# Whole stores, two queues of units and four unequal zero transfers at the end of a decode step's backward pass

## The chip, the cores and the metric

The kernel runs on one core of a Trainium2 chip. The core has five instruction queues that run side by side and meet only at semaphores: TensorE (PE, matrix products; its weight loads are listed apart as PEld), VectorE (DVE), ScalarE (ACT), GpSimd (POOL) and SyncE (SP). All five can ask for DMA transfers, and the transfers run on 16 DMA engines, which move data between the chip's main memory (HBM, here "dram") and the core's on-chip memory (SBUF). PE writes its results to PSUM, from where DVE or ACT copies them to SBUF; such a copy is called an eviction here.

The metric is the device time of one execution in microseconds: the median of several executions. The kernel before has 450.68 us, from three executions between 450.56 and 451.15.

## The reference

The reference is one decode step (one token, batch 1) through two layers that share their weights, and its gradients. Cut to what matters:

```python
def _A_ref(x, k_cache, v_cache, wq, wo):            # attention over the last W = 4096 cache rows
    q = (x @ wq).reshape(1, 1, 32, 128)             # 32 heads, 4 groups of the cache, 8 heads for each
    k = k_cache[:, :, Sk - W:, :]; v = v_cache[:, :, Sk - W:, :]      # Sk = 32768
    p = softmax(q k^T * 128 ** -0.5)
    return (p v).reshape(1, 1, 4096) @ wo

def _B_ref(x, w1, b1, w2):                          # MLP, 1024 -> 3584 -> 1024
    h = x @ w1 + b1
    return (h * tanh(softplus(h))) @ w2

x = x + _A_ref(_layernorm(x), ...); x = x + _B_ref(_layernorm(x), ...)
x = x + _A_ref(_layernorm(x), ...); x = x + _B_ref(_layernorm(x), ...)

_out, _vjp = jax.vjp(f, A_x, A_k_cache, A_v_cache, A_wq, A_wo, B_w1, B_b1, B_w2)
return (_out, *_vjp(grad_out))
```

There are nine outputs, all in bf16: out_0 is the step's result, out_1 the gradient of x, out_2 and out_3 those of the key and value caches (4 groups x 32768 rows x 128 each), out_4 that of wq (1024 x 4096), out_5 of wo (4096 x 1024), out_6 of w1 (1024 x 3584), out_7 of b1 and out_8 of w2 (3584 x 1024). In out_2 and out_3 only the last 4096 rows of each group are computed; the 28672 rows before them are zeros, which the kernel has to write. With two tokens' worth of vectors (one for each layer's pass), the gradient of a weight matrix is a sum of two outer products.

## The kernel before, in words

**The passes.** The kernel first runs the four layers forward, then backward. Since there is one token, every product is a matrix times a vector, and the weights are streamed through the chip: wq and wo as tiles of 128 x 4096 bf16 (1 MB), w2 likewise, w1 kept in SBUF. Tiles go through a ring of eight buffers. `Ring.pump` (L71) issues the load of the next tile on SP as soon as a buffer is free. The last load of the run is that of wq for the backward pass of the first attention layer, "the last pass of wq": eight tiles, in `attn_bwd`, whose loop calls the hook `dn1(t)` after tile t.

**The zeros.** `zeros(n)` (L265) takes n pieces from the list `zjobs` and issues each as a transfer on POOL. A piece is 128 partitions x 4096 bf16, that is 128 rows of 8 KB, 1 MB, from the tile `zt`, which holds zeros. The calls stand at chosen places of the passes, most of them behind a tiny POOL copy (L260) that waits for a value of that place. The last calls are `zeros(4)` in `dp1` and `dq1`, `zeros(2)` in `dn1` at t = 3, and `zeros(4)` behind `attn_bwd`; the last piece of the list is a half.

**Rows for the outer products.** The vectors are needed as rows in one partition each, in `ROWS` (in the memory of w1, no longer needed then): partitions 0 and 1 for wq's gradient, 32 and 33 for wo's, 64 and 65 for w1's, 96 and 97 for w2's. Some are put to HBM earlier (`put_by`) and fetched by POOL with `take_back` (L836), others are turned by PE and ACT (`rowize`, and `rowize_f` for b1's gradient) and sent into place by `rows_go` (L1041), on POOL for three of them and on SP for the last. `twins` (L1070) copies them on SP to the partitions 32 away, into `TWIN`, so that PE can take two products from two sets of partitions.

**The units.** A unit (`unit_dw`) is one or two outer products 128 x 512 into one of four PSUM tiles `wide` (L1078) and one eviction by DVE (L313) or ACT (L316), whichever has the smaller sum of estimated costs, into a staging buffer of 128 x 4096. `units_rows` and `units_cols` are generators that yield after each unit; `units_kv` does the same for the computed cache rows with 32-row products (L1129). They stand in four queues `todo[0]` to `todo[3]`, and `work(n)` takes n units from the queues in turn. All units run after the last pass of wq: 16 units, the end of the gradient of x (`g0_rest`) and the two small stores out_0 and out_1, 32 units, and then the rest with the cache gradients mixed in.

**The stores.** After each unit `store` decides whether to issue a transfer on SP. With a full buffer it stores what is not yet sent (L1050). For the first eight buffers, for the last buffer of each matrix and for all cache buffers it also sends the first half as soon as it is there (L1055). A buffer that was sent goes back to `stage_free`.

**Semaphores of transfers.** Eight semaphores serve SP's transfers in turn and eight POOL's, so the issue of a transfer also waits until the one eight places before it has landed.

Of the kernel before, what the change touches and what calls it, by code (L numbers as in the profile page):

```python
# [15 lines left out]
P = 128  # L16
HQ = 32
DH = 128
# [3 lines left out]
G = 4  # L22
# [71 lines left out]
def kernel(  # L94
# [943 lines left out]
    def rows_go(queue):  # L1038

        while rows_out:  # L1040
            queue.dma_start(*rows_out.pop(0))  # L1041


    def store(dst, s, old, new, of, last):


        h = (of + 1) // 2
        if new == of:
            lo = sent.pop(id(s), 0)
            nc.sync.dma_start(dst[:, lo * 512:], s[:, lo * 512:of * 512])  # L1050
            stage_free.append(s)
        elif old < h <= new and wide and (last or len(firsts) < 8):
            firsts.append(0)
            sent[id(s)] = new
            nc.sync.dma_start(dst[:, 0:new * 512], s[:, 0:new * 512])  # L1055

    sent, firsts = {}, []

    def rooms(left):

# [23 lines left out]
    def units_rows(base, nblk, out):  # L1084

        for c in range(nblk // 4):
            s = stage_free.popleft()
            for tt in range(4):
                n = 0
                while n < 2:  # L1090
                    m = unit_dw(base, NOFF + (4 * c + tt) * P, 512 * n, s[:, tt * D + n * 512:(tt + 1) * D], 2 - n)
                    n += m
                    store(out.rearrange("(c p k) d -> p c (k d)", p=P, k=4)[:, c], s, 2 * tt + n - m, 2 * tt + n, 8,
                          c == nblk // 4 - 1)
                    yield

    def units_cols(base, ncol, out):

        for t in range(TD):
            s = stage_free.popleft()  # L1100
            n = 0
            while n < ncol:
                m = unit_dw(base, t * P, NOFF + 512 * n, s[:, n * 512:ncol * 512], ncol - n)
                n += m
                store(out[t * P:(t + 1) * P, :], s, n - m, n, ncol, t == TD - 1)
                yield

    def kv_rows(a, X, Y, YS):
# [13 lines left out]
    def units_kv(a, g, YS, out_t):  # L1122
        s = stage_free.popleft()
        q = 0
        while q < 8:
            b, m = rooms(8 - q)
            for k in range(2 * m):
                tp = 2 * q + k
                nc.tensor.matmul(b[:, k * 256:(k + 1) * 256], lhsT=RT[32 * g:32 * g + 32, a, tp, :],  # L1129
                                 rhs=YS[32 * g:32 * g + 32, :], start=True, stop=True, tile_position=(32 * g, 0))  # L1130
            evac(s[:, q * 512:(q + m) * 512], b[:, 0:512 * m], cost=((0.69, 0.585), (1.23, 0.95))[m - 1])
            q += m
            store(out_t[0, g, ZR:, :].rearrange("(p t) d -> p (t d)", p=P), s, q - m, q, 8, True)
            yield


# [44 lines left out]


    todo[3].append(units_rows(96, TF, out_8))
    todo[2].append(units_cols(64, 7, out_6))
    do1_acc = tmp([P, HQ], FP32, "da")

    def do1(c):
        if c == 1:
            take_back("AC", 96, NOFF, 1)
            take_back("OC", 32, NOFF)  # L1190
            take_back("NB", 64, 0)
            take_back("NA", 0, 0)
        if c == 4:
            y = to_eight(YR, RT.rearrange("p a t s -> p (a t s)")[:, 0:512].bitcast(FP32))
            nc.vector.tensor_tensor(out=x4[:], in0=y, in1=x3[:], op=ALU.add)
        if c == 5:
            rowize(GA, TD, 32, 0)
            rowize(GB, TD, 96, 0)
            rows_go(nc.gpsimd)
            zeros(2)  # L1200
        if c == 6:
            rowize_f()
            rows_go(nc.gpsimd)

    def dp1():
        zeros(4)
# [10 lines left out]
    def dn1(t):  # L1217
# [64 lines left out]
```

## Time and profile before

| | |
|---|---|
| median of 3 executions | 450.68 us |
| the profiled execution: time, span | 450.31 us, 448.5 us |
| mean granted TensorE clock | 0.668 |
| busy of the span | PE 70%, PEld 54%, DVE 58%, ACT 47%, POOL 10% |
| DMA | 181.40 MB, mean 404 GB/s |
| of it on SP's queue q1, on POOL's queue q0 | 122.30 MB, 58.26 MB |
| units' stage | from 334 us to 424 us of the span |
| zero pieces | 55 of 1024 KB and one of 512 KB on POOL, one of 512 KB on SP |

The span is the time from the first to the last record of the profiled execution; 1.8 us of the execution's time lie outside. "Busy" is the time in which an engine works. In the tables of stretches, one line is one stretch of the span: busy time of each engine and, in brackets, the number of instructions; the granted clock of PE; the DMA share, which is the mean busy share of the 16 DMA engines (one engine alone gives 0.06, and two packets of one engine overlap a little, so that a full load shows as 1.01 to 1.03); and GB/s. A line that names SPq is an issue on SP's queue: its start, how long the issue took with all others merged into it, and how many they are.

### The profile page before, as it was taken

How to read it: one execution, taken by the hardware profiler on the slowest of the kernel's cores; microseconds unless marked ns; L12 is line 12 of the kernel's file. 1: busy time of each engine (PE TensorE's matmuls, PEld its weight loads, DVE VectorE, ACT ScalarE, POOL GpSimd, SP SyncE). 2: the span in 40 equal slices, each digit the busy share in tenths (PEclk: the TensorE clock that was granted, in tenths of full speed). 3: DMA queues.
4: the chain of work that ended last, by engine and by line, in shares of the span. 5: the costliest groups of instructions: out<-in, count | busy, mean ns of one | idle time of the engine just before them, and what ended most of it. 6: DMA issues, size and time to landing. Idle time of an engine off the chain costs nothing.

```text
span 448.5 us, 12849 instructions
## 1 busy us (share of the span) xinstructions
PE 314.8 (70%) x5681; PEld 243.3 (54%) x5681; DVE 262.2 (58%) x516; ACT 209.4 (47%) x238; POOL 44.5 (10%) x94
## 2 busy tenths in 40 slices
PE   3835542565698797987987666798877888899600
PEld 3735532445685696986986545798862222234300
DVE  4504746368551664864477447654478998998600
ACT  2501101011058576861474341561348999999700
POOL 1000000001232212102101003023220000000000
PEclk9955555556559799986799657957685555555555
DMA  8999999999999999999999999999999899999994
GB/s 336 422 420 420 419 419 418 418 355 425 400 422 421 422 422 416 397 422 422 424 422 422 427 423 419 405 410 388 405 397 412 347 411 416 416 420 411 409 406 192
DMA packets 30057, 181.40 MB, mean 404 GB/s; under 512 B 3954, under 2 KB 5162, under 8 KB 12082
## 3 DMA queue, kind: packets, MB, share of 16 engines
q1 hardware_dynamic: 21478, 122.30, 66.6%
q0 software_dynamic: 8432, 58.26, 31.5%
q8 instruction: 44, 0.72, 0.6%
q14 instruction: 11, 0.09, 0.0%
q10 hardware_dynamic: 92, 0.02, 0.0%
HBM read 81.84 MB, written 98.62 MB: 402 GB/s over the span
## 4 chain that ended last, share of the span: by engine, by line
DMA 40%; PE 31%; DVE 13%; ACT 5%; issue 4%; SPq 0%; ACTq 0%; DVEq 0%
DMA ring<-in_B_w_dram 13%; PE BIG L489 10%; DMA W<-in_A_wo_dram 9%; DMA ring<-in_A_wq_dram 7%; DMA ring<-in_A_wo_dram 5%; DMA W<-in_B_w_dram 4%; PE TP L508 4%; PE wide L1129 4%; ACT ring L316 3%; PE wide L1078 3%; DVE ring L313 3%; DMA W<-in_A_k_cache_dram 2%; DVE W L313 2%; PE BIG L667 2%; PE MV L956 2%
## 5 line engine op out<-in xcount | busy, mean ns | idle before, releaser
L316 ACT COPY ring<-BIG 128x1024 bf16<-128x1024 bf16 x52 | 51.4, 1014 | 50.0 <-PE BIG L489 30.2
L1078 PE MATMUL wide<-W 2*128 2x512 bf16 x240 | 53.1, 597 | 9.7 <-ACT ring L316 2.4
L489 PE MATMUL BIG<-ident_bf,ring 128*128 128x128 bf16 x672 | 54.5, 234 | 2.0 <-issue 1.2
L489 PEld LDWEIGHTS <-ring 128*128 128x128 bf16 x768 | 51.6, 107 | 3.4 <-issue 2.7
L466 DVE CUSTOM_DVE_ANT_0 junk<-ring,SC 128x1024 bf16<-128x1024 bf16 x32 | 38.9, 1215 | 11.0 <-DMA ring<-in_B_w_dram 10.6
L1078 PEld LDWEIGHTS <-W 2*128 2x128 bf16 x240 | 12.8, 102 | 46.3 <-issue 45.4
L508 PEld LDWEIGHTS <-ring 128*128 128x128 bf16 x864 | 29.9, 98 | 11.7 <-issue 6.3
L316 ACT CAST ring<-wide 128x1024 bf16<-128x1024 f32 (+1 forms) x37 | 34.5, 1015 | 1.1 <-PE wide L1078 1.1
L265 POOL DMA_DIRECT2D out_dram<-zt x56 | 29.9, 538 | 48.8 <-DMA out_dram<-zt 47.9
L313 DVE CAST ring<-wide 128x1024 bf16<-128x1024 f32 (+1 forms) x27 | 31.3, 1198 | 2.8 <-PE wide L1078 2.7
L316 ACT COPY KT<-BIG 128x1024 bf16<-128x1024 bf16 x22 | 21.6, 1007 | 21.8 <-PE BIG L667 19.9
L313 DVE COPY ring<-BIG 128x1024 bf16<-128x1024 bf16 x32 | 21.8, 689 | 15.1 <-PE BIG L489 12.5
L466 DVE CUSTOM_DVE_ANT_0 junk<-ring,DSX 128x1024 bf16<-128x1024 bf16 x24 | 29.4, 1224 | 0.8
L489 PE MATMUL BIG<-ident_bf,W 128*128 128x128 bf16 x280 | 26.9, 255 | 3.1 <-DMA W<-in_A_wo_dram 2.7
L316 ACT COPY W<-BIG 128x1024 bf16<-128x1024 bf16 x20 | 20.1, 1014 | 11.8 <-PE BIG L489 11.6
L551 PE MATMUL MV<-NA,ring 128*128 128x1 bf16 x512 | 15.3, 165 | 13.4 <-DMA ring<-in_A_wq_dram 12.1
L489 PEld LDWEIGHTS <-W 128*128 128x128 bf16 x288 | 21.6, 123 | 3.5 <-DMA W<-in_A_wo_dram 2.9
L551 PEld LDWEIGHTS <-ring 128*128 128x128 bf16 x512 | 14.7, 104 | 14.2 <-DMA ring<-in_A_wq_dram 12.8
L1129 PE MATMUL wide<-W 32*128 32x256 bf16 x128 | 19.7, 403 | 1.5 <-DVE KT L313 0.9
L316 ACT CAST KT<-wide 128x1024 bf16<-128x1024 f32 x19 | 19.1, 1030 | 1.6 <-PE wide L1129 1.1
L316 ACT CAST W<-wide 128x1024 bf16<-128x1024 f32 x16 | 16.0, 1024 | 6.6 <-PE wide L1078 6.2
L354 PE MATMUL YR<-ring,AC 128*32 128x256 bf16 x208 | 10.9, 367 | 11.1 <-DMA ring<-in_B_w_dram 8.7
(279 smaller groups left out, 524.5 us busy)
## 6 DMA issues: line engine op xcount, KB each, us to landing
out_dram<-zt POOLq DMA_DIRECT2D x55, 1024.0 KB, 20.7
ring<-in_A_wq_dram SPq DMA_DIRECT2D x24, 1024.0 KB, 12.8
ring<-in_A_wo_dram SPq DMA_DIRECT2D x14, 1024.0 KB, 19.0
ring<-in_B_w_dram SPq DMA_DIRECT2D x13, 1024.0 KB, 18.9
W<-in_A_wo_dram SPq DMA_DIRECT2D x10, 1024.0 KB, 19.9
out_dram<-ring SPq DMA_DIRECT2D x15, 512.0 KB, 11.1
W<-in_B_w_dram SPq DMA_DIRECT2D x8, 896.0 KB, 18.4
out_dram<-ring SPq DMA_DIRECT2D x5, 1024.0 KB, 12.3
```

The source lines that it names most:

```text
L265: nc.gpsimd.dma_start(dst, zt[:, 0:dst.shape[1]])
L313: nc.vector.tensor_copy(dst, src)
L316: nc.scalar.copy(dst, src)
L354: nc.tensor.matmul(bank[32 * j:32 * j + 32, 0:n].rearrange("p (g a) -> p g a", a=m.shape[-1]), lhsT=vec.to_broadcast([P, 32]), rhs=m, star ...
L466: nc.vector.tensor_tensor_reduce(out=out, in0=a, in1=vec, scale=1.0, scalar=acc if i else 0.0, op0=ALU.mult, op1=ALU.add, accum_out=acc)
L489: nc.tensor.transpose(b[:, i * P:(i + 1) * P], block(w, i) if block else w[:, i * P:(i + 1) * P], ident_bf[:])
L508: nc.tensor.matmul(out, lhsT=w[:, i * P:(i + 1) * P], rhs=rhs_of(i), start=fresh[0], stop=last and i == n - 1, skip_group_check=True)
L551: nc.tensor.matmul(q_ps[:, h:h + 1], lhsT=ch[:, h * P:(h + 1) * P], rhs=NA[:, t, l:l + 1], start=(k == 0 and h == 0), stop=(k == TD - 1), ...
L667: nc.tensor.transpose(b[:, i * P:(i + 1) * P], T[:, g, 8 * b8 + i, :], ident_bf[:])
L956: nc.tensor.matmul(dq_ps[:, g_ * 8:g_ * 8 + 8], lhsT=KT[:, g_, t, :], rhs=DSX[:, c:c + 8], start=(g_ == 0 and t == 0), stop=(t == TS - 1), ...
L1078: nc.tensor.matmul(b[:, 512 * i:512 * i + 512], lhsT=R[at:at + 2, lo:lo + P], rhs=R[at:at + 2, ro + 512 * i:ro + 512 * i + 512], start=Tru ...
L1129: nc.tensor.matmul(b[:, k * 256:(k + 1) * 256], lhsT=RT[32 * g:32 * g + 32, a, tp, :], rhs=YS[32 * g:32 * g + 32, :], start=True, stop=Tru ...
```

## The change

Five things are changed.

1. `store` issues one transfer for each buffer, when it is full. The halves of before (the lists `sent` and `firsts`) are gone. The buffers, the units and their evictions stay.
2. w1's units follow w2's in `todo[3]`, and wq's units follow wo's in `todo[1]`; before, each of the four matrices had a queue of its own. So SP's order becomes out_5, out_8, out_5, out_8 and so on, and then out_4 and out_6 in turn.
3. The last four zero pieces (512 rows of 8 KB, at the end of the last group of out_3) become four transfers of 132, 17, 99 and 264 rows. Their sources are 4, 1, 3 and 8 single partitions of `zt`, each read 33 times (the single one 17 times). They are issued where `zeros(4)` stood. The other pieces of that group are now each one contiguous block of HBM.
4. `take_back` issues one transfer for each of the two rows of a vector, and for the one of 28 blocks (`AC`) two, of 24 and 4 blocks: ten transfers on POOL, where there were five.
5. `rows_go` for b1's gradient rows (two transfers of 7 x 512) uses SP's queue, ahead of the twins, and not POOL's.

```diff
     zjobs = []
     for out_t in (out_2, out_3):
         for g in range(G):
-            dst = out_t[0, g, 0:ZR, :].rearrange("(p r) d -> p (r d)", p=P).rearrange("p (r c) -> p r c", c=ZC)
-            for k in range(dst.shape[1]):
-                zjobs.append(dst[:, k, :])
+            rest = out_t[0, g, 0:ZR, :]
+            if (out_t, g) != (out_3, G - 1):
+                dst = rest.rearrange("(p r) d -> p (r d)", p=P).rearrange("p (r c) -> p r c", c=ZC)
+            else:
+                units = rest.rearrange("(u r) d -> u (r d)", r=ZC // DH)
+                zless, dst = units[0:4 * P], units[4 * P:].rearrange("(r p) c -> p r c", p=P)
+            zjobs += [dst[:, k, :] for k in range(dst.shape[1])]
...
+    def zeros_less():
+        at = 0
+        for k, p, n in ((4, 0, 33), (1, 16, 17), (3, 20, 33), (8, 64, 33)):
+            nc.gpsimd.dma_start(zless[at:at + k * n].rearrange("(k n) c -> k n c", k=k),
+                                zt[p:p + 4 * k:4, None, :].to_broadcast([k, n, ZC]))
+            at += k * n
...
-    def take_back(name, base, off, step=2):
+    def take_back(name, base, off):
         r = DR[name][:].rearrange("(n l) p -> l n p", l=2)
-        to = ROWS[base:base + 2, off:off + r.shape[1] * P].rearrange("l (n p) -> l n p", p=P)
-        for l in range(0, 2, step):
-            nc.gpsimd.dma_start(to[l:l + step], r[l:l + step])
+        n = r.shape[1]
+        for l in range(2):
+            to = ROWS[base + l:base + l + 1, off:off + n * P].rearrange("o (n p) -> o n p", p=P)
+            for a, b in ((0, 24), (24, n)) if n == TF else ((0, n),):
+                nc.gpsimd.dma_start(to[:, a:b], r[l:l + 1, a:b])
...
-    def store(dst, s, old, new, of, last):
-        h = (of + 1) // 2
+    def store(dst, s, new, of):
         if new == of:
-            lo = sent.pop(id(s), 0)
-            nc.sync.dma_start(dst[:, lo * 512:], s[:, lo * 512:of * 512])
+            nc.sync.dma_start(dst, s[:, 0:of * 512])
             stage_free.append(s)
-        elif old < h <= new and wide and (last or len(firsts) < 8):
-            firsts.append(0)
-            sent[id(s)] = new
-            nc.sync.dma_start(dst[:, 0:new * 512], s[:, 0:new * 512])
...
-    todo[2].append(units_cols(64, 7, out_6))
+    todo[3].append(units_cols(64, 7, out_6))
...
             rowize_f()
-            rows_go(nc.gpsimd)
+            rows_go(nc.sync)
...
-            todo[0].append(units_cols(0, 8, out_4))
+            todo[1].append(units_cols(0, 8, out_4))
...
     g0_rest = attn_bwd(0, sA0, g1, ("o", 3), ("q", 3), (), dict(do=do1, dp=dp1, dq=dq1, dn=dn1))
-    zeros(4)
+    zeros_less()
```

More of the change, by code (lines that the diff above doesn't have):

```diff
@@ L1041, in rows_go @@
             queue.dma_start(*rows_out.pop(0))
-    def store(dst, s, old, new, of, last):
-        h = (of + 1) // 2
+    def store(dst, s, new, of):
         if new == of:
-            lo = sent.pop(id(s), 0)
-            nc.sync.dma_start(dst[:, lo * 512:], s[:, lo * 512:of * 512])
+            nc.sync.dma_start(dst, s[:, 0:of * 512])
             stage_free.append(s)
-        elif old < h <= new and wide and (last or len(firsts) < 8):
-            firsts.append(0)
-            sent[id(s)] = new
-            nc.sync.dma_start(dst[:, 0:new * 512], s[:, 0:new * 512])
-    sent, firsts = {}, []
     def rooms(left):
@@ L1092, in units_rows @@
                     n += m
-                    store(out.rearrange("(c p k) d -> p c (k d)", p=P, k=4)[:, c], s, 2 * tt + n - m, 2 * tt + n, 8,
-                          c == nblk // 4 - 1)
+                    store(out.rearrange("(c p k) d -> p c (k d)", p=P, k=4)[:, c], s, 2 * tt + n, 8)
                     yield
@@ L1104, in units_cols @@
                 n += m
-                store(out[t * P:(t + 1) * P, :], s, n - m, n, ncol, t == TD - 1)
+                store(out[t * P:(t + 1) * P, :], s, n, ncol)
                 yield
@@ L1132, in units_kv @@
             q += m
-            store(out_t[0, g, ZR:, :].rearrange("(p t) d -> p (t d)", p=P), s, q - m, q, 8, True)
+            store(out_t[0, g, ZR:, :].rearrange("(p t) d -> p (t d)", p=P), s, q, 8)
             yield
@@ L1188, in do1 @@
         if c == 1:
-            take_back("AC", 96, NOFF, 1)
+            take_back("AC", 96, NOFF)
             take_back("OC", 32, NOFF)
```

## The prediction

> **What bounds the kernel now.** I read the page's second part first, the span in 40 slices:
>
> ```profile
> DMA  8999999999999999999999999999999899999994
> GB/s 336 422 420 420 419 419 418 418 355 425 400 422 421 422 422 416 397 422 422 424 422 422 427 423 419 405 410 388 405 397 412 347 411 416 416 420 411 409 406 192
> ```
>
> The DMA engines are full from the second slice to the last but one, while no compute engine is above 70%. So bytes and their spread over the 16 engines set the time. In the part that the change touches three places are left to look at: the dip in slice 32, the rate, and the last slice. I asked for stretches of the last 110 us:
>
> ```profile
> 343.00:353.00 10.00, 7.64 (x38) 2.06 (x39) 8.20 (x11) 8.43 (x12) 0.00 (x0) 0.50 1.02 406
> 353.00:357.00 4.00, 2.91 (x18) 0.69 (x14) 4.00 (x4) 3.98 (x5) 0.00 (x0) 0.50 0.62 244
> 357.00:410.00 53.00, 46.34 (x242) 15.15 (x242) 47.42 (x47) 49.93 (x55) 0.00 (x0) 0.50 1.01 416
> 410.00:424.00 14.00, 12.21 (x86) 7.24 (x79) 11.27 (x10) 12.84 (x14) 0.00 (x0) 0.50 1.02 406
> 424.00:442.00 18.00, 0.00 (x0) 0.00 (x0) 0.00 (x0) 0.00 (x0) 0.00 (x0) 0.50 1.02 408
> ```
>
> The last columns are DMA share and GB/s. Compute ends at 424, and 18 us of stores are left: production is not the bound. Between 353 and 357 the share is 0.62, a loss of 0.38 x 4 = 1.5 us of all engines. Then the end, finer:
>
> ```profile
> 441.50:442.00 0.50, 0.00 (x0) 0.00 (x0) 0.00 (x0) 0.00 (x0) 0.00 (x0) 0.50 1.02 401
> 442.00:442.50 0.50, 0.00 (x0) 0.00 (x0) 0.00 (x0) 0.00 (x0) 0.00 (x0) 0.50 0.52 205
> 442.50:443.00 0.50, 0.00 (x0) 0.00 (x0) 0.00 (x0) 0.00 (x0) 0.00 (x0) 0.50 0.14 57
> 443.00:443.50 0.50, 0.00 (x0) 0.00 (x0) 0.00 (x0) 0.00 (x0) 0.00 (x0) 0.50 0.06 25
> 445.00:446.00 1.00, 0.00 (x0) 0.00 (x0) 0.00 (x0) 0.00 (x0) 0.00 (x0) 0.50 0.06 25
> 446.00:447.00 1.00, 0.00 (x0) 0.00 (x0) 0.00 (x0) 0.00 (x0) 0.00 (x0) 0.50 0.07 29
> 447.00:448.50 1.50, 0.00 (x0) 0.00 (x0) 0.00 (x0) 0.00 (x0) 0.00 (x0) 0.50 0.00 0
> ```
>
> A share of 0.06 is one engine of 16. Fifteen engines end near 442.2, one goes on alone to about 447.1: it is 4.9 us late, and the whole kernel waits for it. The trace's records of when each sixteenth of a store landed show one late sixteenth for every store from 356 us to the end, 5 to 6 us behind the first; in the zero queue it lags 6 to 14 us from 186 us on. And it never pauses: followed backwards from its last packet, nearly each packet starts 3 or 4 ns before the one before it ends, back to 335 us, through the dip too. So the late engine's own list of work is the critical path; the dip costs the other fifteen, not it.
>
> Last, what made the dip:
>
> ```profile
> 342.11 3.79 SPq L1050 DMA_DIRECT2D out_dram<-W  x3
> 349.60 0.33 SPq L1050 DMA_DIRECT2D out_dram<-ring  x1
> 353.26 4.23 SPq L1055 DMA_DIRECT2D out_dram<-ring  x4
> ```
>
> ```profile
> SPq L1050 <- DMA out_dram<-W: 4.7, 2, 3.6
> SPq L1055 <- DMA out_dram<-W: 3.3, 1, 3.3
> ```
>
> SP stood still from 345.9 to 349.6 and to 353.3, although the evictions went on: an issue waits until the store some eight transfers before it has landed on all engines, the late one included. Six to eight half stores in flight are 3 to 4 MB, 7 to 10 us of DMA.
>
> **The change part by part.** The sum is made against the profiled execution, 450.31 us; the median is 0.37 above it.
>
> *Unequal zeros.* 512 rows of 8 KB are now 32 for each engine. If each of the 4 + 1 + 3 + 8 = 16 source partitions is one engine's share, fifteen engines get 33 and one gets 17. One engine moves 416/16 = 26 GB/s (stretch 357 to 410; alone it shows 25 to 29), so 8 KB take 0.315 us. The favoured engine saves 15 x 0.315 = 4.7 us, the others lose 0.3. If the favoured one is the late one, its end moves from 447.1 to 442.4. If it is another, the late end moves to 447.4. No row of before shows how a transfer with few leading rows is spread, so both ends stay: -4.7 and +0.3. I take -4.7, because the number fits: 4.9 us of lateness is 15.6 such rows, and 15 are taken. As to which engine it is, the trace says a little: the late engine's chain holds one of the eight packets of 256 B of out_0 and of out_1 each and, less surely, one of the seven of 1 KB of out_7. So if leading rows go to engines in order it is among the first seven, where the single row stands fifth.
>
> [...]
>
> *Whole stores.* 39 transfers where there were 60. Rate: the stretches with mostly half stores (343 to 353, 410 to 442) show 406 to 408 GB/s, the one with mostly whole ones 416. 42 us at 2.2% are 0.9 us. Bounds: 0 (the slower rate could come from the cache rows' own stores) and 0.9; I take 0.7, as both of the rows before and after 424, with and without compute beside, are alike. It counts for every engine, the late one too. Cover: a first store now waits for a full buffer. With two queues the first two are full after 7 and 8 units, 2 MB; before, four halves were ready after 5 to 8 units, 2 MB too, the first at 337.6. The delay of about a unit (0.56 us from the evictions' 1.22 and 1.03 us on two engines) is hidden by the zero queue, which fills the engines until 345. Eight whole stores in flight are 8 MB, so the wait on the first one's semaphore comes only at the ninth, after 39 units, some 15 us later than before: the dip goes. That gives the other fifteen 1.5 us and the late engine nothing. At the end, the last four buffers (4.2 MB) go out only when each is full, near 424: 10 us of DMA and some 2 us of delay, done by 436, behind the backlog that lasts to 442. Without that backlog, they would be the end.
>
> *Two queues.* The same evictions and products. Consecutive units now take partitions 32/0 and 96/64 in turn; before, two neighbours used the same pair. PE is busy 46.3 of 53 us and the evictions 47.4 and 49.9, so a unit can become a little quicker; nothing on the path, as compute ends 18 us early. Bounds: 0 and 0.
>
> *take_back and b1's rows.* Five more issues on POOL at 0.56 us (its row: 0.56 to 0.60 each), 2.8 us, at 277 us, where POOL then idles 18.4 us before the next transfers. The ninth and tenth need the first two to land, in the row 14.8 us later, 292, still before 298. Queued behind them on POOL are the rows at 298.2 and the zeros at 300.3. On SP two issues of up to 1 us each stand ahead of the twins at 305.2; the twins wait for the other rows anyhow, until 317, the longest of these waits being for b1's rows, whose landing takes 11.7 us on POOL and 7.1 us for the like on SP. Units need them at 334. If this cover failed, PE's units would start later, into 18 us of slack. 0 on the path; bounds 0 and +0.3 for a little more work on the late engine.
>
> Sum for the late engine: -4.7 - 0.7 = -5.4, end at 441.7. The others: 442.2 + 0.3 - 0.7 - 1.5 = 440.3. The late one is still last, by 1.4 us. 450.31 - 5.4 = 444.9, and the median 445.3.
>
> **The rivals.** *Another engine is last, or only part of the lateness is removed.* If the dip stays (lanes or first stores), the others end at 441.8, no loss. If the lateness is redistributed by the small transfers or by instruction fetches (44 packets of 16 KB, about 1 us each), one engine may be 1 to 4 us later: 446.4 to 449.6, say 448.
>
> *It helps the wrong engine.* +0.3 - 0.7: 450.3. In the same place: *it does not do what it says*, the rows being dealt evenly over 16 engines; rounding up per transfer gives 9 + 2 + 7 + 17 = 35 rows on the first ones, +0.9 - 0.7: 450.9.
>
> *Slower: production becomes the bound.* A product of the units takes 0.597 us, two per unit, and PE keeps ahead of 0.56 us per unit only by running products of different partitions side by side. If the new order of pairs spoils that, and a unit takes 0.65 us, 162 units end 15 us later, at 439; the last four whole buffers then add 12 us: 451 instead of 447.1, 454.2 in all. It decides from about 12 us of delay (13% per unit). Against it: neighbouring units now use different partitions, not the same.
>
> **How the numbers follow.** The main case, 444.2 to 446.4, has 0.62; part of the lateness left (446.4 to 449.6) 0.14; wrong engine or no spread 0.10, within 0.2% of before, which is 0.9 us and about what three executions of this kernel can tell from no change; slower 0.14. Below 444 there is little: it needs the full 0.9 and an engine whose lateness was smaller. The range runs from 444.0, past the part and up to the wrong engine, 450.2.
>
> **What would show it.** Right: in the last 6 us the share falls from 1.0 to 0 within 2 us, without a stretch of 0.06; no dip at 353 to 357; whole stores only, near 416 GB/s from 357 on; compute still ends more than 10 us before the stores. Wrong: a single engine alone for 5 us again, or compute that ends with the last store. The prediction fails if the late engine is not the one with 17 rows.

## The result, and the profile after

The changed kernel is slower by 0.3%: 451.85 us (median of 18 executions, 451.17 to 454.13) against 450.60 for the kernel before (18 executions, 449.76 to 451.82, taken together). The ratio is 1.0031, with an interval from 1.0022 to 1.0039. The forecast was 445.3. The profiled execution of the changed kernel took 452.31 us, with a span of 450.5.

The page's two rows for the DMA engines and the rate, in 40 slices as before:

```profile
DMA  8999999999999999999999999999999999999992
GB/s 329 423 420 418 421 420 419 418 356 425 396 421 399 402 407 412 398 401 414 423 423 424 422 423 380 417 417 420 421 390 398 397 418 423 415 420 416 420 422 114
```

The dip that stood in slice 32 is gone, but three slices in a row, the 30th to the 32nd (about 327 to 360 us), stay below 400 GB/s. The same stretches as were asked of before (DMA share and GB/s last):

```profile
334.00:341.00 7.00, 5.74 (x30) 1.13 (x23) 6.67 (x6) 6.94 (x8) 0.00 (x0) 0.50 0.98 374
343.00:353.00 10.00, 7.13 (x37) 1.66 (x38) 7.75 (x10) 8.61 (x11) 0.00 (x0) 0.50 1.01 393
353.00:357.00 4.00, 3.54 (x18) 0.85 (x18) 3.82 (x4) 4.00 (x5) 0.00 (x0) 0.50 0.98 389
357.00:410.00 53.00, 46.51 (x238) 15.54 (x236) 47.35 (x45) 49.01 (x56) 0.00 (x0) 0.50 1.01 419
424.00:442.00 18.00, 0.00 (x0) 0.00 (x0) 0.00 (x0) 0.39 (x1) 0.00 (x0) 0.50 0.96 402
441.00:442.00 1.00, 0.00 (x0) 0.00 (x0) 0.00 (x0) 0.00 (x0) 0.00 (x0) 0.50 0.45 188
442.00:444.00 2.00, 0.00 (x0) 0.00 (x0) 0.00 (x0) 0.00 (x0) 0.00 (x0) 0.50 0.26 111
446.00:447.00 1.00, 0.00 (x0) 0.00 (x0) 0.00 (x0) 0.00 (x0) 0.00 (x0) 0.50 0.12 49
448.00:449.00 1.00, 0.00 (x0) 0.00 (x0) 0.00 (x0) 0.00 (x0) 0.00 (x0) 0.50 0.06 25
```

From 353 to 357 the share is 0.98, where it was 0.62, and from 357 on the rate is 419 in place of 416: the whole stores did what they should. Compute still ends near 424. But between 334 and 357 the engines are nearly full and move only 374 to 393 GB/s (before: 414 from 334 to 341, 406 from 343 to 353), so packets take longer or carry less. And the end is worse than before. Then, fifteen engines ended near 442.2 and one at 447.1; now seven are busy on average between 441 and 442 (0.45 x 16), about four between 442 and 444 (0.26 x 16), two at 446, and the last ends at 449. The last engine is later than before, not earlier.

### The profile page after: what moved, and what is told of

Same layout as the page of the kernel before. It is cut to its first block, busy times and chain, and to the rows that moved or that the text cites. A ratio compares the mean times of both kernels' runs of the same rounds, so it can differ in the third digit from the quotient of the medians.

```text
span 450.5 us, 12837 instructions
## 1 busy us (share of the span) xinstructions
PE 312.1 (69%) x5681; PEld 240.5 (53%) x5681; DVE 262.0 (58%) x515; ACT 208.4 (46%) x239; POOL 46.3 (10%) x97
## 4 chain that ended last, share of the span: by engine, by line
PE 37%; DMA 29%; DVE 14%; ACT 8%; issue 6%; SPq 0%; ACTq 0%; DVEq 0%
DMA ring<-in_B_w_dram 13%; PE BIG L502 11%; DMA ring<-in_A_wq_dram 5%; DMA W<-in_A_wo_dram 4%; DVE junk L479 4%; ACT ring L329 4%; PE TP L521 4%; DMA W<-in_B_w_dram 4%; PE wide L1085 4%; PE wide L1135 4%; PE BIG L680 3%; DMA W<-in_A_k_cache_dram 2%; DVE W L326 2%; PE YR L367 2%; DVE KT L326 2%
## 5 line engine op out<-in xcount | busy, mean ns | idle before, releaser
L1085 PE MATMUL wide<-W 2*128 2x512 bf16 x240 | 55.7, 595 | 11.5 <-ACT ring L329 3.0
L329 ACT CAST ring<-wide 128x1024 bf16<-128x1024 f32 (+1 forms) x40 | 36.6, 1047 | 2.6 <-PE wide L1135 1.3
L269 POOL DMA_DIRECT2D out_dram<-zt x52 | 27.7, 537 | 34.2 <-DMA out_dram<-zt 33.4
L326 DVE CAST ring<-wide 128x1024 bf16<-128x1024 f32 (+1 forms) x24 | 27.8, 1197 | 4.4 <-PE wide L1085 2.8
L502 PE MATMUL BIG<-ident_bf,W 128*128 128x128 bf16 x280 | 24.9, 241 | 2.0 <-issue 1.8
L1135 PE MATMUL wide<-W 32*128 32x256 bf16 x128 | 23.0, 404 | 0.9 <-ACT ring L329 0.5
L502 PEld LDWEIGHTS <-W 128*128 128x128 bf16 x288 | 20.0, 115 | 2.7 <-issue 2.7
L329 ACT CAST VS<-wide 128x1024 bf16<-128x1024 f32 (+1 forms) x21 | 19.1, 1001 | 2.2 <-PE wide L1135 1.4
L326 DVE CAST KT<-wide 128x1024 bf16<-128x1024 f32 (+1 forms) x17 | 19.2, 1185 | 1.0 <-issue 0.6
```

Of the source, the lines that this page charges most:

```text
L326: nc.vector.tensor_copy(dst, src)
L329: nc.scalar.copy(dst, src)
L502: nc.tensor.transpose(b[:, i * P:(i + 1) * P], block(w, i) if block else w[:, i * P:(i + 1) * P], ident_bf[:])
L1085: nc.tensor.matmul(b[:, 512 * i:512 * i + 512], lhsT=R[at:at + 2, lo:lo + P], rhs=R[at:at + 2, ro + 512 * i:ro + 512 * i + 512], start=Tru ...
```

## The experiments

All kernels differ from the kernel after, unless the text says so. Each is set against runs of the kernel before on the same chip.

| run | last 512 zero rows: partitions x rows, in order of issue | median, us | ratio to before, interval |
|---|---|---|---|
| the change | 4 x 33, 1 x 17, 3 x 33, 8 x 33 | 451.85 | 1.0031 [1.0022, 1.0039] |
| equal_zeros | four pieces of 128 x 1 | 449.59 | 0.9980 [0.9968, 0.9991] |
| whole_stores (on before) | as before | 450.04 | 0.9992 [0.9981, 1.0004] |
| whole_two_queues (on before) | as before | 449.80 | 0.9982 [0.9972, 0.9992] |
| single_as_eighth | 4 x 33, 3 x 33, 1 x 17, 8 x 33 | 450.66 | 0.9997 [0.9989, 1.0006] |
| eight_singles | eight of 1 x 17 to 113, 16 x 1 | 481.4 | one execution |
| one_partition | 1 x 512 | 587.4 | one execution |
| sixteen_by_32 | 16 x 32 | 456.95 | 1.0139 [1.0120, 1.0159] |
| own_partitions | seven of 4 to 128, x 1 | 451.43 | 1.0026 [1.0005, 1.0046] |
| before_unequal (on before) | as the change | 457.87 | 1.0159 [1.0136, 1.0181] |
| pair_01 | 2 x 11, 6 x 35, 8 x 35 | 450.72 | 0.9996 [0.9986, 1.0006] |
| pair_23 | 2 x 35, 2 x 11, 4 x 35, 8 x 35 | 450.72 | 1.0002 [0.9991, 1.0012] |
| pair_45 | 4 x 35, 2 x 11, 2 x 35, 8 x 35 | 445.58 | 0.9877 [0.9853, 0.9901] |
| pair_67 | 6 x 35, 2 x 11, 8 x 35 | 450.41 | 0.9993 [0.9983, 1.0002] |
| single_5th | 4 x 22, 12 x 6, 5 x 11, 11 x 27 | 445.62 | 0.9890 [0.9875, 0.9905] |
| single_6th | 5 x 22, 11 x 6, 6 x 11, 10 x 27 | 450.17 | 0.9987 [0.9974, 1.0000] |
| no_17 | 4 x 33, 3 x 33, 8 x 33 | 450.26 | 0.9990 [0.9977, 1.0004] |
| two_for_5th | 4 x 33, 12 x 1, 5 x 1, 11 x 33 | 451.06 | 1.0015 [0.9997, 1.0034] |
| before_single_5th (on before) | as single_5th | 459.47 | 1.0206 [1.0191, 1.0221] |

### Which part costs: the parts alone

The change with its four unequal transfers turned back into four equal pieces, and with them the layout of that group's other pieces:

```diff
-            if (out_t, g) != (out_3, G - 1):
+            if True:
...
-    zeros_less()
+    zeros(4)
```

> The changed kernel with its last four zero pieces put back to 128 rows of 8 KB each, 32 for every engine; all else as changed. Theory M (the relief missed): the four unequal transfers helped an engine that was not late, and gave the late one 33 rows, which its chain of packets shows at 0.39 us each, where a row of the old pieces takes 0.315. Then equal pieces take 33 x 0.39 - 32 x 0.315 = 2.8 us from the late engine: about 449.0 us, faster than before. Rival R (the relief worked and something else of the change costs time): the late engine gets 15 rows back, 15 x 0.315 = 4.7 us, and the time rises to about 456.

Measured 449.59. This is near theory M's 449.0 and far from rival R's 456. The stretches that were slow, and the end of this kernel:

```profile
334.00:341.00 7.00, 5.51 (x28) 1.33 (x28) 6.08 (x10) 6.01 (x7) 0.00 (x0) 0.50 1.01 411
341.00:350.00 9.00, 5.79 (x30) 1.66 (x28) 6.56 (x11) 7.05 (x10) 0.00 (x0) 0.50 1.02 418
439.00:440.00 1.00, 0.00 (x0) 0.00 (x0) 0.00 (x0) 0.00 (x0) 0.00 (x0) 0.50 0.22 90
442.00:444.00 2.00, 0.00 (x0) 0.00 (x0) 0.00 (x0) 0.00 (x0) 0.00 (x0) 0.50 0.06 25
444.00:446.00 2.00, 0.00 (x0) 0.00 (x0) 0.00 (x0) 0.00 (x0) 0.00 (x0) 0.50 0.07 29
```

The rate is back at 411 and 418, the others end near 439, and one engine runs alone from 440 to 446. So the unequal transfers cost 2.3 us in place of bringing 4.7, and the late engine of the kernel before is still there. The rest of the change brings 0.2% (450.7 to 449.6).

Of that rest, whole stores alone, and whole stores with two queues, each on the kernel before:

```diff
-        elif old < h <= new and wide and (last or len(firsts) < 8):
+        elif False:
```

```diff
-    todo[2].append(units_cols(64, 7, out_6))
+    todo[3].append(units_cols(64, 7, out_6))
...
-            todo[0].append(units_cols(0, 8, out_4))
+            todo[1].append(units_cols(0, 8, out_4))
```

> The kernel before with whole stores only (four queues of units, old zeros, old rows). Theory M: whole stores are a gain, as the late engine's chain of packets from 334 us on shows 97.0 us of store packets before and 95.4 after the change: 450.6 - 1.5 = about 449.1. Rival R: whole stores are what costs the time, since four buffers fill at the same pace and nothing is ready for 16 units; the engines run dry, the late one too, and it gets slower than 451.6.

> The kernel before with whole stores and two queues of units, nothing else. Theory M: 449.1 like whole stores alone or a little less; the end shows one or two engines alone for several us. Rival R (the order of the units costs time): over 451.6. If it equals the changed kernel with equal zeros, the rows for the outer products (their five more transfers on POOL, and b1's on SP) cost nothing.

450.04 and 449.80: -0.4 us with an interval that takes in 0, and -0.8 us, both less than the 1.5 expected. The second is the same as equal_zeros within the intervals (half a us to either side), so no cost or gain of take_back and b1's rows shows.

### How the rows are dealt

The same four transfers in another order, with the single partition after the three:

```diff
-        for k, p, n in ((4, 0, 33), (1, 16, 17), (3, 20, 33), (8, 64, 33)):
+        for k, p, n in ((4, 0, 33), (3, 16, 33), (1, 28, 17), (8, 64, 33)):
```

> The changed kernel with the transfers in the order 4, 3, 1, 8 source partitions, so that the one with 17 rows is the eighth and not the fifth. Theory M: in the profile of the change the late engine's last rows end at 360 us, which fits the transfer of three partitions (its last sixteenth lands at 362 us) and not the one of four (351 us), so the late engine is the sixth, seventh or eighth. If it is the eighth, it ends 16 x 0.39 = 6 us earlier and the next one, which ended 0.9 us before it, is last: about 451.0. If it is not, 451.9 as changed. Rival R: the fifth was the late one; it gets 16 rows more and the time rises to about 456 us.

450.66, with one engine alone again to 447.4. The late engine was not relieved here either; whether by its place or by the dealing, this run could not tell. So I took a list of eight transfers of one partition each, with 17, 29, 41, 53, 67, 79, 97 and 113 rows, which, if each were one engine's, would order the engines' ends like steps:

```diff
+        for k, p, n in ((1, 0, 17), (1, 4, 29), (1, 8, 41), (1, 12, 53), (1, 16, 67), (1, 20, 79), (1, 24, 97), (1, 28, 113), (16, 64, 1)):
...
```

> The changed kernel with the last 512 rows of zeros as eight transfers of one source partition each, with 17, 29, 41, 53, 67, 79, 97 and 113 rows, and one of 16 partitions with a row each. Theory O (one leading row is one engine, and the next transfer takes the next engine): eight engines end in steps, at about 439 + (n - 32) x 0.315 to 0.40 us, so the last one goes on alone until 465 to 472 us of the span, and 479 if it is the late one; the step that is 7 to 8 us out of line names the late engine's place among the first eight, and if all steps are in line it is not among them. Rival P (the rows of a transfer are spread over more engines): no such steps, and the end stays near 448.

481.4 us, and no steps. The engines were full, but slow:

```profile
343.00:353.00 10.00, 5.48 (x26) 1.24 (x26) 6.44 (x6) 7.76 (x9) 1.06 (x2) 0.50 0.93 172
353.00:363.00 10.00, 8.84 (x46) 2.54 (x44) 9.22 (x10) 9.92 (x12) 0.00 (x0) 0.50 0.93 195
```

A share of 0.93 is fifteen engines at work, where eight transfers with one engine each would keep eight. Half of the zero rows' packets took 0.9 us and more in the trace, not 0.315. The next three kernels ask for the reason: all 512 rows from one partition, then from sixteen, then in unequal numbers but without reading a partition twice in a transfer.

```diff
+        for k, p, n in ((1, 0, 512),):
```

> The last 512 rows of zeros are one transfer that reads a single partition 512 times, in place of the four; the rest is the kernel after. Theory O, the rows of one source partition are one engine's: one engine gets 512 rows where it had 32 to 33, the others none; (512 - 33) x 0.315 us = 151 us behind the late engine's end at 449, so near 600 us, with a share of 0.06 alone for over 130 us. Theory C, rows are dealt over all 16 engines whatever their partition, and many engines that read one partition hinder each other (the eight one-partition transfers moved 143 to 225 GB/s with full engines, and lost 30 us): all engines are slowed together, 32 rows each at 0.9 to 1.3 us, so 20 to 35 us more, 470 to 490, no long stretch at 0.06, and rows that take over 0.8 us each. Theory E, dealt over all engines and the partition plays no part: 449.6, as with equal pieces.

```profile
355.00:365.00 10.00, 0.00 (x0) 0.00 (x0) 0.46 (x1) 0.00 (x0) 0.00 (x0) 0.50 0.94 26
405.00:425.00 20.00, 1.16 (x9) 0.27 (x10) 0.69 (x1) 1.18 (x2) 0.00 (x0) 0.50 0.95 27
```

587 us lies near the time that I had given for "one engine", and it would have been read so without the lines: the share is 0.94 to 0.95, all engines at work, and together they move 26 to 27 GB/s, as much as one engine alone at the end of the kernel before. A row takes 4.68 us, some 15 times 0.315. So this transfer of one partition was dealt to all engines, and they queued for that partition's 27 GB/s. The size that I gave for this (20 to 35 us more) was too small by over 100, since I had taken the rate from eight partitions.

```diff
+        for k, p, n in ((16, 0, 32),):
```

> The last 512 rows are one transfer of 16 partitions, each read 32 times; the number of rows is equal for all engines by any dealing. If reading one partition again and again is slow by itself (0.39 to 0.41 us for a row of the unequal transfers on the late engine, against 0.315), 32 x 0.085 = 2.7 us on each engine: 452.3. If it is slow only where several engines read the same partition, and each engine has a partition of its own here: 449.6, as with equal pieces. If engines are dealt the rows in turn, so that all 16 read the same partition at once: more than with the 1, 3, 4 and 8 partitions, at least 453.

```profile
334.00:341.00 7.00, 5.70 (x27) 1.51 (x25) 6.88 (x7) 7.00 (x9) 0.00 (x0) 0.50 1.01 251
341.00:350.00 9.00, 4.92 (x27) 1.27 (x28) 6.07 (x10) 6.46 (x9) 0.00 (x0) 0.50 0.98 241
```

456.95. Most packets took 0.61 to 0.65 us (0.64 in the median), twice 0.315, and the full engines moved 241 to 251 GB/s, as much as nine sources of 27 GB/s, though sixteen partitions are read (0, 4, 8 to 60). The times fit two engines at each source. That several partitions share one source, and which of them do, is the author's estimate from these rates: no run here tried it.

```diff
+        for n in (128, 4, 17, 99, 128, 128, 8):
+            nc.gpsimd.dma_start(zless[at:at + n], zt[0:n, :])
+            at += n
```

> The last 512 rows in unequal transfers (128, 4, 17, 99, 128, 128 and 8 rows), each row from a partition of its own as in the pieces before them, so that no partition is read twice in a transfer. If what the unequal transfers cost is the reading of few partitions by many engines (theory C): the cost goes, 449.4 to 449.9, and rows take 0.315 us. If it is their unequal number of rows per engine: up to 17 - 8 = some rows more on the first engines, near 451; if it is the layout of that group's other pieces (one block of 1 MB each) or the packets of 4 B that came with them: 451.9 as after.

451.43, and 350 GB/s from 334 to 341. Rows were slow here too (0.375 us on average in this stretch, 0.319 in equal_zeros), so reading a partition again and again is not needed for that. How its transfers of 4, 8, 17 and 99 rows were dealt can be told only from the number of packets, below.

```profile
334.00:341.00 7.00, 5.70 (x29) 1.17 (x24) 6.88 (x6) 7.00 (x9) 1.60 (x3) 0.50 1.01 350
```

### Which engine is late

If a transfer of one partition is an exception, transfers of two and more may still be dealt by partition. Four kernels without a one-partition transfer each give 11 rows to two neighbouring places and 35 to the other fourteen:

```diff
+        for k, p, n in ((2, 0, 11), (6, 8, 35), (8, 64, 35)):                    # pair_01
+        for k, p, n in ((2, 0, 35), (2, 8, 11), (4, 16, 35), (8, 64, 35)):       # pair_23
+        for k, p, n in ((4, 0, 35), (2, 16, 11), (2, 24, 35), (8, 64, 35)):      # pair_45
+        for k, p, n in ((6, 0, 35), (2, 24, 11), (8, 64, 35)):                   # pair_67
```

> No one-partition transfer: the last 512 rows are transfers of 2 partitions x 11, 6 x 35 and 8 x 35 rows. Against equal pieces (449.6, late engine's end near 446, the others' near 439) the engines of the first two partitions get 21 rows less and the others 3 more. Theory D, each partition's rows are one engine's, the first transfer's on the first engines and the next ones' behind them: if the late engine is first or second, 21 x 0.315 = 6.6 us less for it, and the others, at 440, are the end: 443.5 to 445; if it is another, 3 x 0.315 = 0.9 us more: 450.5. Theory C, rows are dealt evenly: about 449.6, the same as the other three pairs. If reading a partition again and again is slow by itself, 452 or more.

> As pair_01 with the 11 rows for the third and fourth place (2 x 35, 2 x 11, 4 x 35, 8 x 35). Theory D: 443.5 to 445 if the late engine stands there, else 450.5. Theory C: 449.6.

> As pair_01 with the 11 rows for the fifth and sixth place (4 x 35, 2 x 11, 2 x 35, 8 x 35); the single row of the change stood fifth. Theory D: 443.5 to 445 if the late engine stands there, else 450.5. Theory C: 449.6.

> As pair_01 with the 11 rows for the seventh and eighth place (6 x 35, 2 x 11, 8 x 35). Theory D: 443.5 to 445 if the late engine stands there, else 450.5. If none of the four is below 449, the late engine is one of the last eight, or rows aren't dealt by partition.

Three have 450.4 to 450.7, as expected of the wrong pair, and one has 445.58 (443.5 to 445 was expected of the right one). The end of pair_01, then two stretches of the zeros and the end of pair_45:

```profile
439.00:440.00 1.00, 0.00 (x0) 0.00 (x0) 0.00 (x0) 0.00 (x0) 0.00 (x0) 0.50 0.27 115
442.00:444.00 2.00, 0.00 (x0) 0.00 (x0) 0.00 (x0) 0.00 (x0) 0.00 (x0) 0.50 0.06 25
444.00:447.00 3.00, 0.00 (x0) 0.00 (x0) 0.00 (x0) 0.00 (x0) 0.00 (x0) 0.50 0.06 27
```

```profile
334.00:341.00 7.00, 5.13 (x26) 1.22 (x26) 5.98 (x11) 5.64 (x7) 0.00 (x0) 0.50 1.01 385
341.00:350.00 9.00, 5.79 (x30) 1.75 (x30) 6.54 (x11) 7.06 (x10) 0.00 (x0) 0.50 1.02 419
440.00:441.00 1.00, 0.00 (x0) 0.00 (x0) 0.00 (x0) 0.00 (x0) 0.00 (x0) 0.50 0.83 352
441.00:442.00 1.00, 0.00 (x0) 0.00 (x0) 0.00 (x0) 0.00 (x0) 0.00 (x0) 0.50 0.18 74
442.00:443.00 1.00, 0.00 (x0) 0.00 (x0) 0.00 (x0) 0.00 (x0) 0.00 (x0) 0.50 0.00 0
```

In pair_45 the share falls from 0.83 to 0 in two us: this is what the prediction said the change would look like. So these transfers of two and more partitions with several rows each were dealt a partition to an engine, each transfer behind the one before, and the late engine is the fifth or sixth. Then 17 rows for one place alone and 33 for the others, which is what the change set out to do, made of transfers that go round the engines twice (22 + 11, 6 + 11 and 6 + 27 rows):

```diff
+        for k, p, n in ((4, 32, 22), (12, 48, 6), (5, 32, 11), (11, 52, 27)):     # single_5th
+        for k, p, n in ((5, 32, 22), (11, 52, 6), (6, 32, 11), (10, 56, 27)):     # single_6th
```

> What the change set out to do, without a transfer of one partition: transfers of 4 x 22, 12 x 6, 5 x 11 and 11 x 27 rows give by theory D (a partition's rows are one engine's, each transfer goes on where the one before ended) 33 rows to every place but the fifth, and 17 to that. If the late engine is the fifth: 15 x 0.315 = 4.7 us less than with equal pieces (449.6), 444.9, or 445.6 as with the pair if other engines are then last. If it is the sixth: 449.6 + 0.3 = 449.9.

> The same for the sixth place (5 x 22, 11 x 6, 6 x 11, 10 x 27 rows). If the late engine is the sixth: 444.9 to 445.6; if it is the fifth: 449.9.

445.62 and 450.17: the late engine is the fifth, the one that the change aimed at. In single_5th the zeros are not slow, though the group's other pieces have the change's layout (so that layout is not what slowed them), and the end is short:

```profile
334.00:341.00 7.00, 4.67 (x23) 1.40 (x20) 6.74 (x11) 5.90 (x8) 0.00 (x0) 0.50 1.02 420
341.00:350.00 9.00, 6.87 (x35) 1.58 (x36) 6.82 (x7) 8.16 (x10) 0.00 (x0) 0.50 1.02 423
438.00:439.00 1.00, 0.00 (x0) 0.00 (x0) 0.00 (x0) 0.00 (x0) 0.00 (x0) 0.50 0.29 123
440.00:442.00 2.00, 0.00 (x0) 0.00 (x0) 0.00 (x0) 0.00 (x0) 0.00 (x0) 0.50 0.06 25
```

One engine is still alone from 440 to 442: of the last store, one sixteenth landed at 442.4 and the others by 440.2, where in equal_zeros it was 446.6 and 440.5. This kernel and pair_45 beat the kernel before by 1.1 and 1.2%, and the kernel after by some 1.4%.

### What the 17 rows do

The change without its transfer of 17 rows, which stay unwritten:

```diff
-        for k, p, n in ((4, 0, 33), (1, 16, 17), (3, 20, 33), (8, 64, 33)):
+        for k, p, n in ((4, 0, 33), (3, 20, 33), (8, 64, 33)):
```

> The change without its transfer of 17 rows from one partition, which are left unwritten (0.14 MB, 0.3 us of all engines); 4, 3 and 8 partitions of 33 rows remain. Theory F, the 17 rows are dealt over many engines that then wait for the one partition (17 rows at 27 GB/s take 5.2 us), and the transfers behind go on at the fifth place: without them the slow rows go, and the fifth place still has its 33 rows and is late by as much as with equal pieces, 449.6 + 0.3 = 449.9; the sixteenth place has none. Theory O, the 17 rows are the fifth place's: without them the next transfers move up by one, the fifth place has 33 rows in place of 17, and the end would be 16 x 0.315 = 5 us later than after, 457.

450.26. If the 17 rows had been the fifth engine's, their absence would have moved the next transfer up and cost 5 us; it made the kernel 1.6 us faster (0.3 of it for the bytes). So the 17 rows were not the fifth engine's and held no place in the order; they only cost. But theory F, which has this, was wrong in one point, the low rates stayed:

```profile
334.00:341.00 7.00, 5.11 (x26) 1.23 (x26) 5.98 (x11) 5.53 (x7) 0.00 (x0) 0.50 0.96 371
341.00:350.00 9.00, 5.71 (x32) 1.76 (x30) 6.56 (x11) 7.06 (x11) 0.00 (x0) 0.50 1.01 381
```

How the 17 rows were dealt can be read from the number of packets on POOL's queue. Its line on the pages of equal_zeros, the change, no_17 and pair_45 (packets, MB, share):

```profile
q0 software_dynamic: 8512, 58.25, 31.6%
q0 software_dynamic: 9616, 58.25, 31.9%
q0 software_dynamic: 9568, 58.11, 31.8%
q0 software_dynamic: 9856, 58.25, 32.2%
```

The bytes are the same (but for the missing rows of no_17), so the packets over 8512 carry no rows; in the traces they have 4 bytes and take 9 ns. All counts come out if one supposes that a transfer ends with one small packet on each of the sixteen engines, and that an engine with fewer rows of it than the others gets a small packet for each row that it lacks. For pair_45 that gives 14 x 11 + (12 + 14 + 8) x 35 = 1344, as counted (9856 - 8512), and for single_5th and single_6th 544, as counted too; for no_17 it is 1089 (below) less the 17 rows and the 16 end packets of the missing transfer, 1056. The transfers of 4, 3 and 8 partitions give 33 x (12 + 13 + 8) = 1089. The change has 1104, so its 17 rows left 15. On one engine they would have left 15 x 17 = 255; with two places on each of the sixteen they leave 32 - 17 = 15. So the 17 rows were shared out, at most two to an engine, and eight_singles (160 more) and own_partitions (96 more) come out in the same way, each number of rows rounded up to a multiple of 16 and 16 end packets for each further transfer. Which engines had the 17 rows the counts do not say.

With the 17 rows out of the order, the eleven partitions behind them go to the engines one place earlier than meant (fifth to fifteenth), so that the fifth has its 33 rows and the sixteenth none. This fits what the expectation of single_as_eighth had read, that the late engine's rows end with the transfer of three partitions. The trace of after shows an engine without rows: of the last zero transfer one sixteenth had landed at 334.5, and the other fifteen landed 13.5 to 37.3 us later.

The low rates have two parts. In the change and in pair_45 it is, from 334 to 341, mostly the small packets: in pair_45, where no partition is shifted, they fill 6.5 of the stretch's 112 engine-us (16 engines, 7 us), in the change 6.3 and in equal_zeros 0.7, while rows take 0.32 us in all three. From 341 to 350 the packets are slow: the stores beside the zeros take 0.343 us in the change and 0.348 in no_17, and 0.311 to 0.315 in equal_zeros, the pairs and the singles. An explanation that fits, an estimate of the author's, is that engines then meet at one source as they seem to in sixteen_by_32, where a row took 0.64 us in place of 0.315. By that estimate the eleven shifted partitions are each read beside another engine's; in single_as_eighth only eight partitions are shifted, and it is 1.2 us faster than the change. This part is argued: the kernel that would settle it, the change with sources moved by one place, was not run, and no run shows which partitions share a source.

Last, whether still fewer rows for the fifth would bring more, and whether the gain stands on the kernel before. The diff is that of the first; the other two are the kernel before with the zero part of the change (the list of pieces and `zeros_less`), once with the transfers of single_5th and once with the change's own:

```diff
+        for k, p, n in ((4, 32, 33), (12, 48, 1), (5, 32, 1), (11, 52, 33)):
```

> 4 x 33, 12 x 1, 5 x 1 and 11 x 33 rows: 34 rows for every place but the fifth, and 2 for that. With 17 rows the fifth engine still ended near 442 and the others near 439. 15 rows less are 4.7 us for it, one more row 0.3 us for the others: the others are the end, near 439.5 to 440.5, and the time 443.0 to 444.5. If another engine is late next, about 445.6 as before.

> The kernel before (halves, four queues) with the same four transfers as single_5th (17 rows for the fifth place, 33 for the others). The fifth engine ends 4.7 us earlier, at 442.5, the others at 442.2 + 0.3: if the zeros' gain stands alone, 445.6 to 446.2. If the halves' stalls come back as in the kernel before with the change's own four transfers (457.9), more than 449.

> The kernel before with the unequal zero transfers alone (halves, four queues and the rows as before). The kernel after lost 2.3 us to equal pieces by them. If that is a cost of the transfers themselves: before + 2.3 = 452.9, and the stretches from 334 to 350 fall below 400 GB/s. If it needs the whole stores (their packets of 8 KB in the same time): 450.6 to 451.5.

The first and the last went another way than expected, and before_single_5th went the second of its two ways (more than 449), by far. two_for_5th has 451.06, with the marks of the change itself, 388 and 380 GB/s and a long end:

```profile
334.00:341.00 7.00, 4.93 (x23) 1.41 (x20) 6.77 (x10) 6.15 (x8) 0.00 (x0) 0.50 0.99 388
341.00:350.00 9.00, 6.61 (x35) 1.59 (x36) 6.78 (x8) 7.90 (x10) 0.00 (x0) 0.50 1.01 380
446.00:448.00 2.00, 0.00 (x0) 0.00 (x0) 0.00 (x0) 0.00 (x0) 0.00 (x0) 0.50 0.12 49
```

Its transfers of 12 and 5 partitions have one row each, so one of their two sizes is 1, as in the transfer of 17 rows. That they held no place either is seen in the landings of its last transfer: one sixteenth at 334.9, the other fifteen from 349.7 to 375.9, so one engine had no rows, and the fifth had 33. How the 12 and the 5 rows were dealt was not seen.

On the kernel before, the same transfers that bring 4 us cost 9 us (459.47), and the change's own cost 7.4 (457.87). The stretches of before_single_5th, and SP's issues in it (start, duration, line; L1063 stores a full buffer or second half, L1068 a first half):

```profile
350.00:357.00 7.00, 5.93 (x31) 1.42 (x29) 6.82 (x7) 6.79 (x9) 0.00 (x0) 0.50 0.73 258
357.00:362.00 5.00, 4.31 (x21) 1.06 (x20) 4.67 (x5) 5.00 (x6) 0.00 (x0) 0.50 0.44 158
362.00:366.00 4.00, 3.78 (x23) 1.39 (x22) 3.16 (x4) 3.72 (x6) 0.00 (x0) 0.50 0.38 150
454.00:456.00 2.00, 0.00 (x0) 0.00 (x0) 0.00 (x0) 0.00 (x0) 0.00 (x0) 0.50 0.06 27
```

```profile
347.42 6.69 SPq L1063 DMA_DIRECT2D out_dram<-W  x3
358.57 0.33 SPq L1063 DMA_DIRECT2D out_dram<-ring  x1
363.99 3.82 SPq L1068 DMA_DIRECT2D out_dram<-ring  x4
```

Its waits in 345 to 368 (us in total, times, longest):

```profile
SPq L1063 <- DMA out_dram<-W: 5.5, 2, 4.4
SPq L1068 <- DMA out_dram<-W: 5.0, 1, 5.0
```

SP issues four stores between 347 and 364, because it waits for earlier stores to land, and the engines run out of work: 0.27 x 7 + 0.56 x 5 + 0.62 x 4 = 7.2 us. The dip of the kernel before (1.5 us) has become five times as costly; with whole stores it does not show. A single engine is alone at the end again, so the late one was not relieved, and rows took 0.35 us on average from 334 to 350 where in single_5th they took 0.31. Both fit a shifted order; why the places would differ on this kernel was not tested. It fetches its rows on POOL in other shapes (parts 4 and 5 of the change); whether these move the places of the zeros behind them, no run shows.

## Why the prediction was wrong

**The step that failed is "Unequal zeros", -4.7, in its condition: "If each of the 4 + 1 + 3 + 8 = 16 source partitions is one engine's share".** No run of before showed that dealing. It held for the transfers of 2 and more partitions with several rows each (445.58 and 450.4 to 450.7 in the four pairs, 445.62 and 450.17 in the two singles) and not for the one partition with 17 rows, the only one that mattered: its rows were shared out over the engines (15 small packets in place of 255), it took no place in the order, and the late engine, the fifth, had 33 rows. The prediction gave as bounds -4.7 and +0.3 and chose by "the number fits"; the number did fit what was meant, and told nothing of what the transfer does. The other bound, +0.3, was wrong too: the rows were priced at 0.315 us wherever they are read, and those that were read last, from 350 us on, took 0.39 on average. Against equal pieces, the step came out at +2.3, of which 1.6 less 0.3 hang on the 17 rows (no_17); the remaining 1.0 is the late engine's 33rd row (0.3) and, as argued above, the slow packets.

The packet counts agree with rows shared out over the engines for the transfers of one partition (17 rows left 15 small packets) and with a partition to an engine for those of several partitions with several rows each (1344 in pair_45, 544 in single_5th). That a shared-out transfer takes no place in the order is an inference, which the engine without rows bears out (in the change, one sixteenth of the last zero transfer landed 13.5 us ahead of the others).

**What held.** The late engine's own list is the path: equal_zeros, which speeds up the others to 439, gained 0.2%, and 15 rows less for one engine gained 4.0 (449.59 to 445.62). The term was -4.7, so even its size was near. The place was right: fifth. The prediction's own sign said only "among the first seven", so that it was the fifth owes something to luck. With that one step mended, the kernel has 445.62 where 445.3 was forecast. The runs show places and not engine numbers: the late engine has the fifth place (445.62 in single_5th), and rows taken from the seventh and eighth (pair_67, 450.41) did not help.

**Whole stores, -0.7.** -0.4 alone (interval from -0.9 to +0.2) and -0.8 with two queues; the rate in 357 to 410 rose from 416 to 419. The dip went, as forecast. (The stores of before are 59, not 60.) **Two queues, 0**: within the intervals. **take_back and b1's rows, 0**: right as a price. Whether the zeros' gain needs them stays open: before_single_5th, which has neither them nor whole stores nor two queues, took 459.47.

**The rivals.** Nearest came "It helps the wrong engine" with its second half, "the rows being dealt evenly", 450.3 and 450.9, to which I gave 0.10. In kind it was right for one transfer, whose 17 rows it puts at 2 on the first engines, and no rival had slow or empty packets in it, which go with the last us to 451.85. "Production becomes the bound" did not happen: compute ends at 424 as before.

## What to carry to other kernels

One DMA engine of sixteen ended late here, and 15 rows less for it brought 4.0 us (449.59 to 445.62), near the 4.7 that 15 packets of 0.315 us come to; but try the dealing before trusting it, with a number of rows that no other theory gives, on shapes like the real one. A transfer of one partition or of one row for each partition was no way to reach one engine here (451.85 in the change, 451.06 in two_for_5th); transfers of two and more partitions with several rows each were (445.58 in pair_45), and differences between two rounds of such transfers over the engines reached a single one (445.62 in single_5th). Count the packets: packets without rows told how a transfer was dealt (15 for the 17 rows of the change, 1344 in pair_45). Look at GB/s and share together: full engines at 241 to 251 GB/s took 0.64 us for a row in place of 0.315, full engines at 385 spent 6.5 of 112 engine-us on packets without rows, and a time alone would have misled (587 us was near the time expected under the wrong theory).

## What the hardware showed unexpectedly

- All sixteen engines, reading one partition, moved 26 to 27 GB/s together, a row of 8 KB in 4.68 us (one_partition); with sixteen partitions from 0 to 60 in steps of 4 they moved 241 to 251 GB/s (sixteen_by_32).
- The late engine is the fifth in the order in which rows are dealt, in both groups of runs that tried its place (445.58 in pair_45, 445.62 in single_5th). Why it is late was not studied.
- The transfers on POOL with unequal rows came with further packets of 4 bytes, 9 ns each; their numbers fit one for each row that an engine lacks. There are 1344 more of them in pair_45 than in equal_zeros; from 334 to 341 such packets fill 6.5 of 112 engine-us, and the rate there is 385 GB/s (411 in equal_zeros).
- The same four zero transfers that bring 4 us on equal_zeros cost 9 us on the kernel before. Whether its half stores alone do it, or the order on POOL as well, stays open.
